# Hash attention and channel mix on one core: pair 1's preparation on VectorE with joined bits, pairs 2 and 3 with one transposing DMA each, a new order

## The chip, the cores and the metric

The kernel runs on one core of a Trainium2 chip. A core has five engines that run side by side and meet through semaphores: TensorE (PE, matrix products and transposes; its weight loads are shown as PEld), VectorE (DVE), ScalarE (ACT, exponentials and other functions), GpSimd (POOL) and SyncE (SP, which here issues nearly all DMAs). Each engine works through its own instructions in order. PE writes to PSUM, a small memory with eight banks per partition; DVE and ACT read it from there, POOL does not.

The metric is the time of one execution on the device in microseconds (us); lower is better. Three runs are given by their median. A profile is one further execution with the hardware profiler; its times count from the start of its span.

## The reference

There are 4 batches with 8 heads of 768 positions and 64 dimensions. Each row of q and of k gets a bucket: the signs of 6 projections. A score counts only where both buckets are the same. Then follow a softmax, the product with v, and a channel mix ("moe" in the names) over the 512 joined columns:

```python
q_bits = (np.einsum('bhsd,dk->bhsk', q, proj) > 0).astype(np.int64)
k_bits = (np.einsum('bhsd,dk->bhsk', k, proj) > 0).astype(np.int64)
...
mask = q_bucket[:, :, :, None] == k_bucket[:, :, None, :]
scores = scale * np.matmul(q, k.transpose(0, 1, 3, 2))
scores = np.where(mask, scores, -1000000000.0)
...
return np.matmul(attn, v).astype(np.float32)
...
xk = mu_k * x + (1.0 - mu_k) * x_prev
xr = mu_r * x + (1.0 - mu_r) * x_prev
k = np.maximum(xk @ w_k, 0.0)
v = k * k @ w_v
r = 1.0 / (1.0 + np.exp(-(xr @ w_r)))
return (r * v).astype(np.float32)
```

x is the attention output with its heads joined, x_prev is x moved on by one position. The output is float32, 4 x 768 x 512.

## The kernel before

**Pairs.** Two heads make a pair; there are 16 pairs, numbered 0 to 15, four to a batch. For each pair the kernel builds, per side (q or k) and head j, an operand `a` of 128 rows by 768 positions in float16. Its rows 0 to 63 hold four times the value rounded to float16. Its rows 64 to 127 hold, in six of them, a large positive or negative number for each of the six bits, so that the product of a q and a k column is large where all bits agree, and the exponential of any other is nothing. In pairs that are split into two float16 parts, rows 64 to 127 first get the rounded-off part ("lo"), and the six rows of bits are written over it.

**Two ways to prepare a pair.** The function `add_prep_turn` (the "turned" way) serves pairs 0 and 1. Per side: `hi` (L467, DVE) rounds to float16 into the tile `nh`; `y` (L478, PE) transposes the float32 input into PSUM; `ey` (L483, ACT) copies it out; `x` (L489, PE) multiplies it by the projection in float32; `ex` (L497, DVE) turns the results into signs inside `nh`; `t` (L512, PE, one per head) transposes `nh` into PSUM and `evt` (L517 on DVE, L519 on ACT) copies it into `a`. Pair 0 goes head by head, pair 1 with both heads of a side at once. The rest of `nh` is zero, from the memset `nz` (L265).

The function `add_prep` serves pairs 2 to 15: `hi` (L398, DVE), `lo` (L401, DVE), then a transposing DMA `tr` (L405, SP) writes `a`. Pairs 2 and 3 do this side by side (`hi2q`, `hi2k` and so on), pairs 4 to 15 (`MERGED`) with one tile for q and k together. Then `add_bits` makes the bits of all four blocks (q and k, two heads) jointly: `bits` (L427, PE, 16 products from `a`), `bx` (L431, DVE, takes the sign from PSUM into a tile), and four copies `row` (L443, POOL), one per side and head, which put six rows of bits into `a`. A score needs the rows of its own head from q and from k.

**Scores and the rest.** The scores of a pair are cut into nine steps of 1024 columns: `sc` (L544, PE) into PSUM, `exp` (L548, ACT) from there into `pt`. Steps 0 to 3 belong to head 0, step 4 to both, 5 to 8 to head 1; the order may take them in any sequence. `oo` (L571, PE, three parts per head) multiplies by v, `rc` and `ob` (L582 to L589, DVE) divide, `ot` (L599, PE) or a DMA (L605) turns the result, and the mix (L630 to L646, DVE) follows. When a batch's four pairs are mixed, its channel mix runs: `kp` (L659, PE), Relu (L663, ACT), square (L666, DVE), `r` (L679, PE) with a tanh (L682, ACT), `v` (L692, PE, two halves of four products), the last product (L699, DVE) and the store (L702, SP). v is loaded by SP (`ldv`, L335) and summed on POOL (L350 to L362); q and k by `ldq` (L330, for pair 0 L321).

**The order.** Each piece of work is added to a plan with its engine, what it reads and writes, and a PSUM bank if it takes one. The list `ORDER` then gives the sequence in which all 1332 pieces are issued, and with it the sequence on each engine and on SP's and ACT's DMA queues; the list `BANKS` gives each piece its PSUM bank. Both were written out by hand or by a planner ahead of time; nothing is reordered on the chip. Four score steps can be held in PSUM at once, fewer while other work holds banks.

At the start PE is given work on a zeroed tile until data arrive: `warm` (L246, 14 products of 256 columns) and eight `warmb` (L251, two products each), some of which stand later in the order.

Of the kernel before, what the change touches and what calls it, by code (L numbers as in the profile page):

```python
# [8 lines left out]
FP32 = mybir.dt.float32  # L9
FP16 = mybir.dt.float16  # L10
# [59 lines left out]
]  # L70

BANKS = [
# [56 lines left out]
def kernel(  # L129
# [13 lines left out]
    nc = tc.nc  # L143
# [5 lines left out]
    P = 128  # L149
# [629 lines left out]
```

## Time and profile before

| | us |
|---|---|
| median of 3 runs | 243.06 (242.08 to 243.22) |
| the profiled execution | 242.0 |
| its span, first to last instruction | 240.2 |
| busy: PE / ACT / DVE / POOL | 234.1 / 181.9 / 179.8 / 99.7 |

The granted TensorE clock was 1.00. HBM read 24.12 MB and written 6.29 MB.

In the profile's rows a group shows the line, the engine, the operation, the tiles out<-in by the program's names, and how often; then times in us (mean of one in ns). In a timeline a row shows the start, the time until the last one of the group ends, and in brackets the idle time of the engine before it and what ended it. PE's products overlap, so a row of PE ends after the next has begun. Some of PE's records can be missing from a trace. A DMA row on SP is the time of its issue; the time to landing is given in the DMA view.

### The profile page before, as it was taken

To read this page: it belongs to the slowest core of one execution; us is meant where nothing else is said; L and a number is where in the kernel's file an instruction comes from. 1 tells how busy PE (TensorE), PEld (TensorE's weight loads), DVE (VectorE), ACT (ScalarE), POOL (GpSimd) and SP (SyncE) were. 2 spreads that over 40 slices of the span, in tenths; PEclk is the share of its full clock that TensorE was granted. 3 is DMA by queue.
4 is the path that set the end of the run, shared out by engine and by line. 5 is a ranking of instruction groups with operands and counts; after the bars stand their busy time and mean duration, and the time that the engine had idled before them with its cause. 6 is when DMAs were issued, how large, how long until landed. Compare 5 with 4: busy or idle time off the path is not lost.

```text
span 240.2 us, 6251 instructions
## 1 busy us (share of the span) xinstructions
PE 234.1 (97%) x2515; PEld 147.8 (62%) x2532; DVE 179.8 (75%) x388; ACT 181.9 (76%) x242; POOL 99.7 (41%) x148
## 2 busy tenths in 40 slices
PE   8999999999999999999999999999999999999994
PEld 6985776776766565656456656665566564455442
DVE  3488789999998898989868896887167867348232
ACT  2699999999999999889779999677884640256320
POOL 4064979989934899438087302550000000000000
PEclk9999999999999999999999999999999999999999
DMA  6989999999999999988999989401500401210333
GB/s 225 304 222 274 232 242 260 279 197 362 279 253 284 273 213 294 249 302 206 276 163 241 249 177 234 136 0 26 173 0 3 120 3 44 87 46 1 131 135 131
DMA packets 72605, 44.00 MB, mean 183 GB/s; under 512 B 54912, under 2 KB 67584, under 8 KB 72576
## 3 DMA queue, kind: packets, MB, share of 16 engines
q1 hardware_dynamic: 72208, 43.20, 70.9%
q8 instruction: 20, 0.33, 0.6%
q10 hardware_dynamic: 368, 0.39, 0.5%
q14 instruction: 9, 0.07, 0.1%
HBM read 24.12 MB, written 6.29 MB: 127 GB/s over the span
## 4 chain that ended last, share of the span: by engine, by line
PE 92%; ACT 5%; issue 1%; DVE 0%
PE ps_all L544 25%; PE ps_all L692 17%; PE ps_all L659 16%; PE ps_all L571 14%; PE ps_all L679 8%; ACT pt L548 4%; PE ps_all L427 4%; PE ps_all L489 2%; PE ps_all L512 1%; PE ps_all L478 1%; ACT kr L663 1%; PE ps_all L251 1%; PE ps_all L246 1%; PE ps_all L599 1%; PE ps_all L566 1%
## 5 line engine op out<-in xcount | busy, mean ns | idle before, releaser
L548 ACT ACTIVATE pt<-ps_all 128x1024 bf16<-128x1024 f32 x144 | 138.4, 1041 | 10.9 <-PE ps_all L544 10.3
L544 PE MATMUL ps_all<-a 128*128 128x256 f16 (+1 forms) x384 | 79.2, 325 | 0.5 <-ACT pt L548 0.3
L443 POOL COPY a<-bx 6x384 f32<-6x384 f32 x56 | 38.9, 695 | 34.4 <-DVE bx L431 19.6
L544 PEld LDWEIGHTS <-a 128*128 128x128 f16 x384 | 34.0, 98 | 23.5 <-issue 4.6
L659 PE MATMUL ps_all<-xk,wk 128*128 128x384 bf16 x256 | 48.3, 326 | 0.1
L571 PEld LDWEIGHTS <-pt 128*128 128x128 bf16 x1152 | 42.5, 97 | 8.0 <-issue 0.5
L692 PE MATMUL ps_all<-wv,k 128*128 128x512 bf16 (+2 forms) x199 | 45.6, 362 | 0.5
L571 PE MATMUL ps_all<-va,pt 128*128 128x65 bf16 x1152 | 44.8, 193 | 0.0
L663 ACT ACTIVATE kr<-ps_all 128x384 bf16<-128x384 f32 x64 | 29.4, 491 | 16.0 <-PE ps_all L659 14.4
L659 PEld LDWEIGHTS <-wk 128*128 128x128 bf16 x256 | 24.2, 98 | 17.0 <-issue 0.6
L692 PEld LDWEIGHTS <-k 128*128 128x128 bf16 x208 | 19.3, 98 | 18.9 <-issue 0.3
L699 DVE SCALAR_TENSOR_TENSOR os<-rs,ps_all 128x512 f32<-128x512 f32 (+2 forms) x26 | 16.5, 643 | 19.0 <-PE ps_all L692 13.7
L682 ACT ACTIVATE rs<-ps_all 128x512 f32<-128x512 f32 x24 | 14.3, 602 | 20.5 <-PE ps_all L679 14.1
L666 DVE TENSOR_TENSOR k<-kr 128x384 bf16<-128x384 bf16 x64 | 23.2, 389 | 8.3 <-ACT kr L663 8.3
L401 DVE SCALAR_TENSOR_TENSOR nh<-nat,nh 128x1536 f16<-128x1536 f32 (+1 forms) x16 | 27.0, 1694 | 0.2
L679 PE MATMUL ps_all<-wr,xr 128*128 128x512 bf16 x88 | 23.2, 379 | 0.4
L356 POOL TENSOR_TENSOR vt<-vn 128x384 f32<-128x384 f32 x12 | 17.8, 1485 | 12.5 <-DMA vn<-in_v_dram 11.7
L589 DVE TENSOR_TENSOR ob<-ps_all,rc 128x384 bf16<-128x384 f32 x32 | 17.5, 553 | 1.4 <-DMA xt<-ob 0.8
L431 DVE TENSOR_SCALAR bx<-ps_all 128x768 uint16<-128x768 uint16 x14 | 13.4, 956 | 5.3 <-PE ps_all L427 4.7
L398 DVE TENSOR_SCALAR nh<-nat 128x1536 f16<-128x1536 f32 (+1 forms) x16 | 15.8, 985 | 0.3 <-PE ps_all L512 0.2
L679 PEld LDWEIGHTS <-xr 128*128 128x128 bf16 x96 | 9.0, 98 | 9.0
L380 DVE SCALAR_TENSOR_TENSOR va<-ps_all,vn 128x384 bf16<-128x384 f32 x24 | 12.7, 548 | 0.5 <-PE ps_all L375 0.2
(77 smaller groups left out, 188.9 us busy)
## 6 DMA issues: line engine op xcount, KB each, us to landing
vn<-in_v_dram SPq DMA_DIRECT2D x16, 384.0 KB, 5.1
out_dram<-os SPq DMA_DIRECT2D x23, 256.0 KB, 2.3
nat<-in_k_dram SPq DMA_DIRECT2D x15, 384.0 KB, 4.7
nat<-in_q_dram SPq DMA_DIRECT2D x15, 384.0 KB, 5.2
wst<-in_moe_w_k_dram SPq DMA_DIRECT2D x2, 512.0 KB, 7.0
wst<-in_moe_w_r_dram SPq DMA_DIRECT2D x2, 512.0 KB, 5.8
wst<-in_moe_w_v_dram SPq DMA_DIRECT2D x2, 512.0 KB, 4.4
k<-in_moe_w_k_dram SPq DMA_DIRECT2D x1, 512.0 KB, 4.4
```

Source lines behind the costliest of these rows:

```text
L356: e.tensor_tensor(out=vt[:, :, :, 0:E], in0=src[:, :, 0:3, 0:E], in1=src[:, :, 3:6, 0:E], op=ALU.add)
L401: nc.vector.scalar_tensor_tensor(out=nh[:, :, D:P], in0=nat.rearrange("p j (c d) -> p (j c) d", d=D), scalar=QS, in1=nh[:, :, 0:D], op0=AL ...
L443: nc.gpsimd.tensor_copy(side_a[side][n % NAQ][D : D + NB, j, :].bitcast(FP32), bx_t[sx][32 * i : 32 * i + NB, :].bitcast(FP32))
L544: nc.tensor.matmul(ps[:, lo - s * STEP : hi - s * STEP], side_a["k"][sa][:, j, jc * P : (jc + 1) * P], side_a["q"][sa][:, j, q0 : q0 + hi ...
L548: nc.scalar.activation(out=pt_t[sp][:, s * STEP : (s + 1) * STEP], in_=ps_t[plan.slot[nm]], func=AF.Exp, bias=EBIAS, scale=ESC)
L571: nc.tensor.matmul(oo[:, ic * 65 : ic * 65 + 65], pt_t[sp][:, o : o + P], va_t[sa][:, j, jc, 0 : D + 1], start=(not uc and ic == 0 and jc ...
L589: nc.vector.tensor_tensor(out=ob_t[so][:, :, j * D : (j + 1) * D], in0=oo[:, :, 0:D], in1=rc_t[sr][:, 1, :].unsqueeze(2).to_broadcast([P, ...
L659: nc.tensor.matmul(ps[:, 0:HALF], wk_sb[:, d, fc * P : (fc + 1) * P], xk_t[mx[d]][:, h * HALF : (h + 1) * HALF], start=(d == 0), stop=(d = ...
L663: nc.scalar.activation(out=kr_t[sk], in_=sm(nm)[:, 0:HALF], func=AF.Relu, scale=0.5 ** 0.5)
L666: nc.vector.tensor_tensor(out=k2_t[s2][:, h * HALF : (h + 1) * HALF], in0=kr_t[sk], in1=kr_t[sk], op=ALU.mult)
L679: nc.tensor.matmul(sm(nr), xr_t[mx[d]][:, c * P : (c + 1) * P], wr_sb[:, d, :], start=(d == 0), stop=(d == NDC - 1))
L692: nc.tensor.matmul(sm(nv)[:, x0:x1], k2_t[(b * NFC + fc) % NK2][:, c * P : (c + 1) * P], wv_sb[:, fc, x0:x1], start=(fc == 0), stop=(fc == ...
```

## The change

1. **Pair 1** leaves `add_prep_turn` (`FIRSTS` is now `(0,)`). It goes through `add_prep` side by side: `hi1q`, `lo1q`, `hi1k`, `lo1k` on DVE (L398, L401). It is in the new set `TURNED`: instead of the transposing DMA, PE transposes each head's `nh` (`t1q0` and so on) and DVE copies it out (`evt1q0` and so on). Its bits now come from `add_bits`: `bits1`, `bx1`, and four copies `row1` on POOL. So the float32 transposes, ACT's copies, the float32 products and the sign steps of pair 1 are gone.
2. **Pairs 2 and 3** join `MERGED`: one `hi`, one `lo` and one transposing DMA each, on a tile of q and k together, where there were two of each.
3. **Opening.** The tile `tb`, its memset on POOL and the small exponential named `table` on ACT are removed; `NWARM` is 8 instead of 14; the second `nh` tile is no longer zeroed; pair 0's transposes no longer name the warm products as something they wait for.
4. **`ORDER` and `BANKS`** are new throughout. The opening, read from the numbers:

```
SP before:  ldq0q0 ldq0q1 ldpw1 ldq1k ldq2k mur ldq2q ldq3k ldq1q ldv0 ldv1 ldq3q tr2q tr2k ldq4k ldv2 ldq4q muk ldv3 tr3q tr3k
SP after:   ldq0q0 ldq0q1 ldpw1 ldq1q mur ldq1k muk ldq2q ldv0 ldq2k ldv1 ldq3q ldv2 ldq3k ldq4k tr2qk ldq4q tr3qk ldv3
DVE before: wz nz0 hi0k0 hi0k1 hi0q0 ex0k0 ex0q0 hi0q1 nz1 evt0q0 ex0k1 hi1k0 ex0q1 hi2k evt0q1 hi2q lo2q lo2k ex1k0 mur hi1q0 evt1k1 hi3k ex1q0 evt1k0 evt1q1 evt1q0 hi3q lo3q bx2 lo3k hi4qk lo4qk
DVE after:  wz hi0q0 nz0 hi0k0 hi0q1 hi0k1 hi1q ex0q0 mur ex0k0 lo1q ex0k1 evt0q0 hi1k ex0q1 lo1k evt1q0 evt0q1 evt1k0 evt1k1 hi2qk evt1q1 lo2qk bx1 hi3qk rc0.0 lo3qk rc0.1 muk ob0.1 ob0.0 bx2 xt0 xs0 df0 hi4qk
PE after:   warm0-5 warmb7 warmb6 warm6 warm7 y0q0 warmb5 y0k1 y0q1 y0k0 warmb3 x0q0 x0k0 warmb2 x0k1 t0k0 t0q0 t0k1 x0q1 sc0_0 sc0_1 t1q0 t0q1 t1k0 sc0_2 t1k1 sc0_7 t1q1 sc0_5 sc0_4 sc0_3 bits1 sc0_8 oo0_0 (two parts) sc0_6 oo0_0 (third) sc1_5 sc1_7 sc1_8 oo0_1 (three) sc1_6 sc1_4 sc1_0 bits2
POOL after: ... va0 vsum0 vsum0b va1 vsum0c (2 memsets) row1k1 row1q1 row1q0 (2 memsets) row1k0 vsum1 va2 ...
```

PE's sequence before is in the timeline rows of the prediction; in the order before, pair 1 opens with score step 8, and pair 0's product with v begins behind six score steps of pair 1. At the end of the kernel the store of row block 4 of the last batch now stands between the stores of 256 to 511 and the last one, columns 0 to 255 of block 5.

The core of the diff (the two number lists left out):

```diff
-    NWARM = 14
+    NWARM = 8
...
-    MERGED = tuple(range(4, 16))
-    FIRSTS = (0, 1)
+    MERGED = tuple(range(2, 16))
+    FIRSTS = (0,)
+    TURNED = (1,)
...
-    tb = buf([P, 2], FP32, "tb")
     add("DVE", 0.2, lambda: nc.vector.memset(wz, 0.0), w=["wz"])
-    add("POOL", 0.1, lambda: nc.gpsimd.memset(tb, 0.0), w=["tb"], port=1, name="ctb")
...
-    add("ACT", 1.5, lambda: nc.scalar.activation(out=tb[:, 0:1], in_=tb[:, 1:2], func=AF.Exp), r=["tb"], w=["tb0"], at=0.75, name="table")
...
-    for i in range(NNH):
+    for i in range(1):
         add("DVE", 0.8, lambda i=i: nc.vector.memset(nh_t[i][:, :, D + NB : P].bitcast(FP32), 0.0), w=[("nz", i)], name=f"nz{i}")
...
             add("DVE", DVE_C(768 * m), lo, r=rn + nh_h, w=nh_l + [("nz", sh)], port=1, name=f"lo{n}")
+            if n in TURNED:
+                for j in range(2):
+                    nm = f"t{n}{side}{j}"
+
+                    def tp(nm=nm, nh=nh, j=j):
+                        ps = sm(nm)[:, 0:HALF].bitcast(FP16)
+                        for c in range(NSC):
+                            nc.tensor.transpose(ps[:, c * P : (c + 1) * P], nh[:, j * NSC + c, :], idh)
+
+                    def ev(nm=nm, a=a, j=j):
+                        nc.vector.tensor_copy(a[:, j, :], sm(nm)[:, 0:HALF].bitcast(FP16))
+                    add("PE", 0.48, tp, r=["idh", ("nhh", side, sh, j), ("nhl", side, sh, j)], w=[(nm,)], take=("sm", nm, 0), name=nm)
+                    add("DVE", DVE_C(S, 2), ev, r=[(nm,)], w=[("a", side, sa, j)] + [("ab", side, sa, j, h) for h in range(2)], give=[nm], name="ev" + nm)
+                continue
             add("SP", 1.86 if whole else 1.46, tr, r=nh_h + nh_l, w=ax, svc=2.95 if whole else 1.57, tr=1, name=f"tr{n}")
...
-                add("PE", 0.06 * 3 * m, tp, r=["idf", "warm", ("pt", 1, 8 * S // STEP)] + rn, w=[(ny,)], take=("sc" if whole else "sm", ny, 0), name=ny)
+                add("PE", 0.06 * 3 * m, tp, r=["idf", ("pt", 1, 8 * S // STEP)] + rn, w=[(ny,)], take=("sc" if whole else "sm", ny, 0), name=ny)
```

119 rows, old and new, of tables (BANKS, ORDER) are left out of this document.

## The prediction, made before the result was known

> **What bounds the kernel now.** I read the page's engine shares first, then the chain of work that ended last, the waits of TensorE and ScalarE, a table of windows, and the timelines of the first 60 us.
>
> ```profile
> PE 234.1 (97%) x2515; PEld 147.8 (62%) x2532; DVE 179.8 (75%) x388; ACT 181.9 (76%) x242; POOL 99.7 (41%) x148
> ...
> PE 92%; ACT 5%; issue 1%; DVE 0%
> ...
> PE ps_all L544 <- ACT pt L548: 0.3, 1, 0.3
> ...
> ACT pt L548 <- PE ps_all L544: 1.1, 4, 0.4
> ...
> 20.90:57.00 36.10, 36.07 (x585) 25.01 (x582) 33.23 (x58) 35.89 (x40) 29.64 (x35) 1.00 1.10 257
> 57.00:99.00 42.00, 41.46 (x525) 27.00 (x520) 39.09 (x82) 41.25 (x56) 32.48 (x37) 1.00 1.13 271
> 99.00:188.00 89.00, 88.47 (x920) 53.18 (x929) 68.71 (x156) 72.01 (x94) 28.03 (x43) 1.00 0.63 157
> ```
>
> TensorE (PE) is busy 234.1 of 240.2 us and has 92% of the chain, so the kernel seems simply bound by it. The windows (length, then busy PE, PEld, DVE, ACT, POOL) say more. From 99 to 188 us PE is full while ACT has 17 us of slack: there the end is set by how much PE work is left. But from 20.9 to 99 us ACT is full as well (35.89 of 36.10, 41.25 of 42.00), and its waits for PE in 19 to 99 us come to 1.1 us. In that stage two engines are full together; a microsecond taken from PE alone makes PE wait for ACT. MoE work that could fill PE needs pair 3, so it cannot come early, and in both orders the same MoE pieces stand ahead of score step 5 of pair 10 (four halves of `v0`, three of `kp1`). The PE work left at that step is the same before and after, so the end moves by what that step moves, and up to there ACT's row of exponentials sets the time:
>
> ```profile
> 10.19 0.81 ACT L483 ACTIVATE pt<-ps_all 128x768 f32<-128x768 f32 x1 [1.08 <-PE ps_all L478]
> ...
> 11.60 4.69 ACT L548 ACTIVATE pt<-ps_all 128x1024 bf16<-128x1024 f32 x5
> ...
> 16.13 0.85 ACT L483 ACTIVATE pt<-ps_all 128x768 f32<-128x768 f32 x1
> ...
> 19.06 35.03 ACT L548 ACTIVATE pt<-ps_all 128x1024 bf16<-128x1024 f32 x38 [0.24 <-PE ps_all L544]
> ```
>
> One step lasts 35.03/38 = 0.92 us. Pair 0 has nine: five in the row at 11.60, two behind the copy at 16.13, two at 19.06. The tenth, the first of pair 1, starts at 19.06 + 2 x 0.92 = 20.9. The question is when it starts after the change.
>
> **The change part by part: PE and ACT.**
>
> ```profile
> 1.59 0.85 PE L246 MATMUL ps_all<-k 128*128 128x256 bf16 x3
> ...
> 4.99 0.38 PE L246 MATMUL ps_all<-k 128*128 128x256 bf16 x2
> ...
> 8.32 0.50 PE L512 MATMUL ps_all<-idh,nh 128*128 128x128 f16 x6
> ...
> 9.30 0.85 PE L478 MATMUL ps_all<-pt,nat 128*128 128x128 f32 x6
> ...
> 10.97 0.59 PE L544 MATMUL ps_all<-a 128*128 128x512 f16 x2
> ...
> 13.59 1.51 PE L489 MATMUL ps_all<-pw,pt 128*128 128x12 f32 x12
> ...
> 14.95 0.85 PE L478 MATMUL ps_all<-pt,nat 128*128 128x128 f32 x6
> ...
> 17.18 1.41 PE L489 MATMUL ps_all<-pw,pt 128*128 128x12 f32 x12
> ...
> 39.64 0.83 PE L427 MATMUL ps_all<-a,p 128*32 128x512 f16 x16
> ```
>
> Pair 1 loses its float32 transposes and bit products: 0.85 + 0.85 + 1.51 + 1.41 = 4.62 us of PE rows, about 4.0 of PE's time since each row's end overlaps the next start by some 0.15. It gains one joined bits step, 0.83. PE is thus relieved of 3.2 us. ACT loses two copies (0.81 and 0.85). Fewer warm matmuls end the filling earlier: twelve fillers at the slow opening rate (0.85 for 3, less the overlap, 0.21 each; two stand ahead of the row at 1.59) end at 1.2 + 2.6 = 3.8, ahead of the next filler row shown; the data of pair 0 then set the start. The removed table operation, the memset of `tb` and the second memset of `nh` I cost at nothing: ACT, POOL and DVE wait for pair 0's data or for PE in the opening (the rows at 10.19 and 15.21 name such waits), and these waits cover them; were that cover gone, DVE's memset would be worth about one `lo` half.
>
> **DVE, where the work goes.** It takes over pair 1's `lo`, and it has everything else of the opening.
>
> ```profile
> nat<-in_k_dram SPq DMA_DIRECT2D x1, 384.0 KB, 4.8
> ...
> 2.27 1.09 SPq L330 DMA_DIRECT2D nat<-in_k_dram  x2
> ...
> 13.08 1.83 DVE L401 SCALAR_TENSOR_TENSOR nh<-nat,nh 128x768 f16<-128x768 f32 x2
> ...
> 15.21 0.23 DVE L497 TENSOR_SCALAR nh<-ps_all 128x72 uint16<-128x72 uint16 x1 [0.30 <-PE ps_all L489]
> 15.36 0.26 DVE L275 TENSOR_SCALAR mur<-mur 128x4 f32<-128x4 f32 x1
> 15.53 0.55 DVE L467 TENSOR_SCALAR nh<-nat 128x768 f16<-128x768 f32 x1
> ...
> 19.52 1.26 DVE L517 COPY a<-ps_all 128x768 f16<-128x768 f16 x2 [0.20 <-PE ps_all L512]
> ...
> 22.49 0.96 DVE L431 TENSOR_SCALAR bx<-ps_all 128x768 uint16<-128x768 uint16 x1 [0.24 <-PE ps_all L427]
> 23.36 0.95 DVE L401 SCALAR_TENSOR_TENSOR nh<-nat,nh 128x768 f16<-128x768 f32 x1
> 24.39 1.10 DVE L398 TENSOR_SCALAR nh<-nat 128x1536 f16<-128x1536 f32 x1
> 25.52 1.94 DVE L401 SCALAR_TENSOR_TENSOR nh<-nat,nh 128x1536 f16<-128x1536 f32 x1
> ```
>
> SP now issues q of pair 1 at 2.27, where k stood; by its row it lands 4.8 later, at 7.1. In DVE's new order `hi1q` waits for that ahead of pair 0's sign steps, so these are late: 0.55, then sign step 0.2, `mur` 0.26, sign step 0.2, `lo1q` 0.92, sign step 0.2, about 9.2 with the overlaps. PE's `t0k1` (0.50 by its row, less the overlap) and `x0q1` (half of 1.41) follow: first scores at 10.3, first exponential 0.63 later as now (10.97 to 11.60), at 10.9. That is 0.7 earlier than now. Pair 0's nine steps end at 10.9 + 9 x 0.92 = 19.2, with no copy of pair 1 between them.
>
> Is pair 1 ready at 19.2? DVE goes on: a sign step behind `x0q1` (10.7), `lo1k` 0.92 (11.6), four copies out of PSUM, the first held by PE until 11.7, at 0.5 each (13.7), `hi2qk`, now whole, 1.10 (14.8), the fifth copy (15.3), `lo2qk` whole 1.94 (17.2), `bx1` 0.96 (18.2). PE's bits step of pair 1 waits only for the fifth copy and is over by 16.4, so DVE alone sets 18.2.
>
> Then POOL copies the bits into rows (L443), and each copy must be done before a score of its head:
>
> ```profile
> 23.58 1.09 POOL L443 COPY a<-bx 6x384 f32<-6x384 f32 x1 [2.77 <-issue]
> 24.73 1.12 POOL L443 COPY a<-bx 6x384 f32<-6x384 f32 x1
> 25.91 1.92 POOL L443 COPY a<-bx 6x384 f32<-6x384 f32 x1
> 27.89 0.50 POOL L443 COPY a<-bx 6x384 f32<-6x384 f32 x1
> ```
>
> The same copy takes 0.50 or up to 1.92, and the DVE rows say when: the first ends at 24.67, 0.36 behind the `lo` that ran beside it (24.31); the second at 25.85, 0.36 behind the `hi` (25.49); the third at 27.83, 0.37 behind the whole `lo` (27.46); the fourth, beside short DVE work, takes 0.50. In the new DVE order `hi3qk` and `lo3qk` stand right behind `bx1`, with one 0.18 reciprocal between. So `hi3qk` 18.2 to 19.3 holds the first row to 19.6, and `lo3qk` 19.4 to 21.3 the second to 21.7. Score step 5 of pair 1, which opens the pair and needs both, starts at 21.7, its exponential at 22.35: 1.45 later than now. ACT stands idle from 19.2, and PE behind its waiting score: its savings are spent there. Bounds for the two rows: both free, 18.3 + 0.50 + 0.50, exponential at 20.1 (-0.8); both at 1.92, 22.9 (+2.0). I take the timed ones, as the trace shows the same neighbours.
>
> **DMA.** Pairs 2 and 3 have one transposing DMA each in place of two.
>
> ```profile
> a<-nh SPq DMA_TRANSPOSE x2, 4.0
> ...
> a<-nh SPq DMA_TRANSPOSE x1, 8.4
> ...
> 28.16 5.02 SPq L405 DMA_TRANSPOSE a<-nh  x1
> ```
>
> Today's halves of pair 2 land 4.0 after issue, a whole one 8.4 (behind loads). The whole one can start only at 17.2, so it lands between 21.2 and 25.6; PE comes to pair 2's bits at about 22.35 + 3 x 0.92 = 25.1, so it is hidden but for up to 0.5, which I keep for the upper end. SP is held 5.0 by that issue; behind it stand `ldq4q`, `tr3qk` and `ldv3`, whose v is needed ahead of pair 3's rows some ten steps later: hidden. In DVE two `hi` halves (1.1) become one (1.1), two `lo` halves 1.83 become 1.94.
>
> **The rest of the order.** Behind the tenth step the counts are the same. I credit 0.5 of ACT's 1.1 us of waits, since PE has pair 0's first head multiplied by v by then. For the new order I add 0.3, the size of the one PE wait for ACT named above (ends: 0 and 1.5, five such). At the end a 256 KB store is issued just ahead of the last one; rows of the stores:
>
> ```profile
> out_dram<-os SPq DMA_DIRECT2D x23, 256.0 KB, 2.3
> ...
> out_dram<-os SPq DMA_DIRECT2D x1, 128.0 KB, 1.7
> ```
>
> Alone, the last lands 1.7 after its issue, a big one 0.6 later than that. With the big one just ahead of it I take 0.2 more, an estimate between 0 and that 0.6.
>
> **Sum:** +1.45 - 0.5 + 0.3 + 0.2 = +1.45 us. The profiled execution took 242.0 (span 240.2); it would be 243.45. It lies 1.06 below the median of the runs, 243.06; on the median I predict 244.5.
>
> **Rivals.** *The PE saving is kept.* The page's 97% speaks for it, the full ACT against it. It decides if pair 1's second row is there by 18.5, when step 5 can follow pair 0 without a gap: the tenth step starts at 19.2, -1.7; with the credit and the store -2.0: 241.1. *It comes out even.* If only one of the two rows is held, 0.50 and 1.12, the exponential starts at 18.3 + 0.5 + 0.1 + 1.1 + 0.1 + 0.6 = 20.7, and with the rest (0) the end moves by -0.2: 242.9. *Pair 2 is late too.* `hi4qk` stands three short operations behind `bx2`; if it holds the second row of pair 2 by its 1.10, ACT waits again: 245.6. *The PE clock falls.* PE stands behind score step 5 from about 18.5 to 21.7, 3.2 us; today no such gap exists and every window has clock 1.00. At the opening, 256 columns took 0.21 at first and 0.11 later, for 3.2 us; if that comes back, 3.2 us of work take twice the time, at least 1.6 of PE: 246.1. The Trainium skill ("TensorE: Matmul & The Clock Gate", What's actually happening) says that an idle window of about 3.4 us throttles PE to half its clock; the estimated gap is just short of it, and no run here shows such a gap.
>
> **How the numbers follow.** A half per cent, 1.2 us, is about what a measurement of this kernel can tell from no change. Late rows (the forecast, 244.5) 0.36; even 0.22; saving kept 0.20; pair 2 late 0.15; clock 0.07. Faster: nearly all of the third case, 0.19. Slower: the last two and seven tenths of the first, 0.47. Same: the rest, 0.34. Range: 241.0 (the saving kept) to 246.8 (rows at 1.92 and a late pair 2).
>
> **What would show it.** Right: first exponential near 10.9, then the ninth ending near 19.2, an ACT gap of 2 to 3 us before L548 ended by PE, row copies of 1.0 to 2.2 us beside `hi` and `lo` of pair 3, and the tenth step near 22.3. Wrong: no ACT gap at 19 us (the saving kept), or PE idle past 99 us, where I see none.

## The result and the profile after

The changed kernel takes 244.02 us (median of 15 executions, 242.32 to 246.19); the kernel before took 242.74 beside it (15 executions, 242.08 to 243.7). The ratio is 1.0051, with a 95% interval of 1.0026 to 1.0075: slower by half a per cent. The profiled execution took 243.99 us, its span is 242.2 (before 242.0 and 240.2), so it is near the median. Two of the 15 executions, 244.82 and 246.19 us, had a mean TensorE clock of 0.993, the other 13 of 0.998 to 1.00; that is one of the prediction's rivals and comes up again below.

The page of the changed kernel, its shares and its chain, and the same windows as before (length, then busy PE, PEld, DVE, ACT, POOL, then the granted clock and the DMA share):

```profile
PE 232.7 (96%) x2490; PEld 144.8 (60%) x2506; DVE 183.9 (76%) x384; ACT 180.3 (74%) x239; POOL 104.2 (43%) x151
...
PE 80%; DMA 10%; DVE 3%; issue 2%; ACT 2%; POOL 1%; SPq 0%; ACTq 0%; DVEq 0%; POOLq 0%
```

```profile
11.60:20.90 9.30, 7.44 (x100) 5.01 (x98) 8.44 (x12) 7.82 (x9) 7.11 (x10) 1.00 0.74 237
20.90:57.00 36.10, 34.93 (x523) 23.75 (x526) 33.09 (x52) 34.96 (x39) 32.88 (x45) 1.00 1.12 254
57.00:99.00 42.00, 41.90 (x545) 27.48 (x540) 39.37 (x86) 41.16 (x56) 30.52 (x35) 1.00 1.09 262
99.00:188.00 89.00, 87.67 (x905) 52.35 (x913) 67.08 (x148) 70.31 (x95) 30.80 (x44) 1.00 0.72 167
```

PE now stands idle for 1.86 us of the stretch from 11.60 to 20.90 and for 1.17 of the one from 20.90 to 57, where before it was full in both. The row of before for the first stretch (that for the second, 36.07 of 36.10, is in the prediction):

```profile
11.60:20.90 9.30, 9.30 (x88) 7.30 (x86) 7.60 (x15) 9.06 (x12) 6.19 (x9) 1.00 0.91 230
```

In the chain PE has 80% (before 92%), and DMA, which had no share of note, has 10% (half of it a load of k, half a transposing DMA). From 99 to 188 us PE is idle for 1.33 (before 0.53), and 0.77 of that is one wait, the last row of PE below.

ACT's opening in the changed kernel (start, time to the end of the row's last, idle before and what ended it):

```profile
11.03 7.48 ACT L559 ACTIVATE pt<-ps_all 128x1024 bf16<-128x1024 f32 x8 [0.24 <-PE ps_all L555]
19.98 1.02 ACT L559 ACTIVATE pt<-ps_all 128x1024 bf16<-128x1024 f32 x1 [1.48 <-PE ps_all L555]
21.47 7.62 ACT L559 ACTIVATE pt<-ps_all 128x1024 bf16<-128x1024 f32 x8 [0.46 <-PE ps_all L555]
```

The first exponential comes at 11.03 (before 11.60). Pair 0's first eight follow in one row, but ACT waits 1.48 for the ninth, and the tenth, pair 1's first, starts at 21.47 where it was 20.89. The other three engines of the changed kernel in that stretch say why:

```profile
15.86 2.27 DVE L398 SCALAR_TENSOR_TENSOR nh<-nat,nh 128x1536 f16<-128x1536 f32 x1
18.05 0.94 DVE L442 TENSOR_SCALAR bx<-ps_all 128x768 uint16<-128x768 uint16 x1
18.92 0.94 DVE L395 TENSOR_SCALAR nh<-nat 128x1536 f16<-128x1536 f32 x1
20.42 0.20 DVE L593 RECIPROCAL rc<-ps_all 128x6 f32<-128x6 f32 x1 [0.56 <-PE ps_all L582]
20.53 1.86 DVE L398 SCALAR_TENSOR_TENSOR nh<-nat,nh 128x1536 f16<-128x1536 f32 x1
```

```profile
16.48 1.92 POOL L359 TENSOR_TENSOR vsu<-vt 128x130 bf16<-128x130 f32 x1
...
19.14 1.09 POOL L454 COPY a<-bx 6x384 f32<-6x384 f32 x1 [0.61 <-DVE bx L442]
20.28 0.50 POOL L454 COPY a<-bx 6x384 f32<-6x384 f32 x1
20.84 1.92 POOL L454 COPY a<-bx 6x384 f32<-6x384 f32 x1
```

```profile
18.45 0.33 PE L577 MATMUL ps_all<-vsu,tiny 128*128 128x390 bf16 x1 [1.09 <-POOL vsu L359]
...
20.84 1.46 PE L555 MATMUL ps_all<-a 128*128 128x256 f16 x8 [0.53 <-POOL a L454]
...
103.45 0.83 PE L438 MATMUL ps_all<-a,p 128*32 128x512 f16 x16 [0.77 <-DMA a<-nh]
```

DVE's whole `lo2qk` (15.86 to 18.13) holds the last small sum over v of pair 0 on POOL (L359, 1.92) until 18.40; the same sum took 0.42 in the timeline of before (L362 there):

```profile
18.47 0.42 POOL L362 TENSOR_TENSOR vsu<-vt 128x130 bf16<-128x130 f32 x1
```

The product with v (L577) waits for it, and score step 6 of pair 0 stands behind that on PE: so the ninth exponential is late. `hi3qk` (to 19.86) holds the first row copy of pair 1 (1.09, to 20.23). The second takes 0.50, because the reciprocal `rc0.0` waited for PE until 20.42 and `lo3qk` could not start before 20.53; the third, which no early score needs, is held to 22.76.

The same opening starts its exponentials at different times in different executions (11.60 in the kernel before, 12.91 in b_wl6, whose opening is the same), so a run is best read from its own first exponential. The table gives, from the trace of every run but b_copies_dve (its opening stalls, see below), the start of the first exponential, then the time from there to the start of the 10th, 46th and 91st exponential and to the end of PE's last product; the last column is the ratio to the kernel before with its interval.

| run | first | 10th | 46th | 91st | PE's end | ratio |
|---|---|---|---|---|---|---|
| before | 11.60 | 9.29 | 42.71 | 96.47 | 225.08 | 1 |
| after | 11.03 | 10.44 | 44.51 | 98.76 | 227.59 | 1.0051 (1.0026 to 1.0075) |
| b_pe_cut | 11.56 | 8.84 | 42.37 | 97.06 | 225.66 | 0.9997 (0.9977 to 1.0017) |
| b_wl6 | 12.91 | 9.29 | 42.71 | 97.57 | 226.18 | 1.0026 (1.0007 to 1.0046) |
| b_merge | 12.28 | 9.29 | 43.64 | 97.78 | 226.38 | 1.0048 (1.0013 to 1.0084) |
| a_bits10 | 10.29 | 10.26 | 44.60 | 99.74 | 228.59 | 1.0049 (1.0019 to 1.0078) |
| a_sc06 | 11.37 | 9.78 | 43.85 | 98.75 | 227.57 | 1.0060 (1.0028 to 1.0091) |
| a_wl6 | 11.20 | 9.46 | 43.55 | 97.56 | 226.39 | 1.0051 (1.0027 to 1.0075) |
| a_wl6_sc06 | 11.04 | 11.45 | 46.52 | 100.52 | 229.35 | 1.0074 (1.0042 to 1.0106) |
| a_hi3 | 11.37 | 8.89 | 44.07 | 98.04 | 226.87 | 1.0026 (1.0005 to 1.0046) |
| a_best | 10.18 | 9.10 | 44.66 | 98.07 | 226.89 | 1.0032 (1.0011 to 1.0053) |
| a_halves | 11.17 | 10.13 | 43.84 | 97.86 | 227.33 | 0.9989 (0.9967 to 1.0012) |
| a_new | 10.42 | 10.09 | 43.83 | 97.24 | 225.88 | 0.9972 (0.9951 to 0.9993) |

Names with a `b` start from the kernel before, those with an `a` from the changed one. Before and after, piece by piece: -0.57 at the first exponential, +1.15 to the tenth, +0.65 to the 46th, +0.49 to the 91st, +0.22 to PE's end: +1.94. That is more than the 1.28 between the medians, since the profiled execution of before (242.0) was one of its faster ones. So in these two traces the changed kernel starts its exponentials earlier and loses four times that behind the first one (2.51 us), nearly half of it by the tenth.

### The profile page after: what moved, and what is told of

Read it like the earlier page. It is cut to its first block, busy times and chain, and to the rows that moved or that the text cites. A ratio compares the mean times of both kernels' runs of the same rounds, so it can differ in the third digit from the quotient of the medians.

```text
span 242.2 us, 6201 instructions
## 1 busy us (share of the span) xinstructions
PE 232.7 (96%) x2490; PEld 144.8 (60%) x2506; DVE 183.9 (76%) x384; ACT 180.3 (74%) x239; POOL 104.2 (43%) x151
## 4 chain that ended last, share of the span: by engine, by line
PE 80%; DMA 10%; DVE 3%; issue 2%; ACT 2%; POOL 1%; SPq 0%; ACTq 0%; DVEq 0%; POOLq 0%
PE ps_all L555 22%; PE ps_all L670 17%; PE ps_all L703 16%; PE ps_all L582 12%; PE ps_all L690 8%; DMA nat<-in_k_dram 5%; DMA a<-nh 5%; PE ps_all L438 4%; ACT pt L559 2%; DVE nh L398 1%; PE ps_all L610 1%; POOL a L454 1%; DVE nh L395 0%; DVE xk L646 0%; DVE bx L442 0%
## 5 line engine op out<-in xcount | busy, mean ns | idle before, releaser
L555 PE MATMUL ps_all<-a 128*128 128x512 f16 (+1 forms) x384 | 79.5, 325 | 1.2 <-POOL a L454 0.5
L454 POOL COPY a<-bx 6x384 f32<-6x384 f32 x60 | 44.2, 736 | 34.0 <-DVE bx L442 17.3
L703 PE MATMUL ps_all<-wv,k 128*128 128x512 bf16 (+2 forms) x200 | 46.1, 362 | 0.4
L677 DVE TENSOR_TENSOR k<-kr 128x384 bf16<-128x384 bf16 x64 | 24.1, 392 | 17.5 <-ACT kr L674 17.4
L398 DVE SCALAR_TENSOR_TENSOR nh<-nat,nh 128x1536 f16<-128x1536 f32 (+1 forms) x16 | 28.4, 1778 | 0.2
L353 POOL TENSOR_TENSOR vt<-vn 128x384 f32<-128x384 f32 x12 | 17.1, 1425 | 9.8 <-DMA vn<-in_v_dram 6.8
L442 DVE TENSOR_SCALAR bx<-ps_all 128x768 uint16<-128x768 uint16 x15 | 14.3, 955 | 3.8 <-PE ps_all L438 2.0
L438 PE MATMUL ps_all<-a,p 128*32 128x256 f16 (+1 forms) x240 | 13.1, 328 | 1.0 <-DMA a<-nh 0.8
```

What stands on the lines that cost most here:

```text
L398: nc.vector.scalar_tensor_tensor(out=nh[:, :, D:P], in0=nat.rearrange("p j (c d) -> p (j c) d", d=D), scalar=QS, in1=nh[:, :, 0:D], op0=AL ...
L438: nc.tensor.matmul(ps[32 * i : 32 * i + 32, lo:hi], w_, side_a[side][m % NAQ][:, j, lo:hi], start=(x == 0), stop=(x == len(mats) - 1))
L454: nc.gpsimd.tensor_copy(side_a[side][n % NAQ][D : D + NB, j, :].bitcast(FP32), bx_t[sx][32 * i : 32 * i + NB, :].bitcast(FP32))
L555: nc.tensor.matmul(ps[:, lo - s * STEP : hi - s * STEP], side_a["k"][sa][:, j, jc * P : (jc + 1) * P], side_a["q"][sa][:, j, q0 : q0 + hi ...
L677: nc.vector.tensor_tensor(out=k2_t[s2][:, h * HALF : (h + 1) * HALF], in0=kr_t[sk], in1=kr_t[sk], op=ALU.mult)
L703: nc.tensor.matmul(sm(nv)[:, x0:x1], k2_t[(b * NFC + fc) % NK2][:, c * P : (c + 1) * P], wv_sb[:, fc, x0:x1], start=(fc == 0), stop=(fc == ...
```

## The experiments

**What TensorE's saving alone is worth.** In the kernel before, pair 1's float32 transposes and bit products are replaced by short bf16 products on the zeroed tile. Pair 1's bits are not computed in this run; everything else is as before. In the expectations of this and the next three runs, W is the prediction's account (ACT's row and the waits around it set the time), P that PE's work sets it.

```diff
 pair 1 of the kernel before, y (L478) and x (L489)
-    six float32 transposes of 128 columns per head; six float32 products of 12 columns per head
+    one bf16 product of 512 and one of 256 columns; one of 12 * NB columns
```

> The kernel before, with pair 1's float32 transposes and bit products each replaced by one or two short bfloat16 products on the zero tile (so pair 1's bits are not computed): about 3.6 us less work on PE, nothing else moved. Theory W (ScalarE's row of exponentials sets the time up to about 99 us, so PE work saved in the opening is mostly lost to waiting): the end moves by -0.4 to -1.0 us, as far as the first exponential moves. Rival P (PE at 97% bounds everything): the end moves by -3.0 to -3.6 us.

Measured: 242.45 us, ratio 0.9997. Neither the 3.0 us of P nor even W's small gain arrived. The tenth exponential is 0.45 earlier, the 46th 0.34, and the 91st 0.59 later than before: PE waits at 94.8 us for pair 9's row copies, which POOL did not have ready. A view of the waits and of the timeline of that run:

```profile
PE ps_all L551 <- POOL a L443: 0.8, 1, 0.8
```

```profile
95.54 1.46 PE L551 MATMUL ps_all<-a 128*128 128x512 f16 x8 [0.75 <-POOL a L443]
```

**Pair 1's copies from ACT to DVE,** to relieve ACT alone:

```diff
-                ("ACT" if n == 0 else "ACT",      # engine of ey
+                ("ACT" if n == 0 else "DVE",
```

> The kernel before, with pair 1's two copies out of PSUM (0.81 and 0.85 us) on VectorE instead of ScalarE; PE work is unchanged. Theory W: ScalarE's row becomes 1.66 us shorter ahead of the tenth step; the end moves by -0.8 to -1.6 us. Rival P: 0, within 0.3 us.

Measured: 248.45 us, ratio 1.0221 (1.0181 to 1.0262), a plain miss. The copy `ey1` stands in DVE's order where its input isn't there yet, and a part of pair 0's preparation is queued behind it. So the run says nothing on ACT, but it shows what a gap on PE costs. Timeline and windows of this run:

```profile
9.93 0.96 DVE L485 TENSOR_SCALAR pt<-ps_all 128x768 f32<-128x768 f32 x1 [1.96 <-PE ps_all L478]
...
12.45 0.51 PE L512 MATMUL ps_all<-idh,nh 128*128 128x128 f16 x6 [2.56 <-DVE nh L497]
```

```profile
10.00:15.00 5.00, 2.55 (x23) 1.88 (x24) 3.97 (x10) 1.73 (x2) 0.32 (x1) 0.92 0.87 311
15.00:20.00 5.00, 5.00 (x35) 3.77 (x34) 4.75 (x7) 3.97 (x5) 4.76 (x7) 0.74 0.28 55
```

PE waits 2.56 us, and its clock falls to a mean of 0.92 and then 0.74 in the two windows shown: the clock rival's mechanism.

**Two waits of the changed kernel, one at a time.** First the late one: PE waits at 102.7 us for pair 10's transposing DMA, with MoE work behind it that could go ahead.

```diff
 PE order of the changed kernel
-  bits10 sc9_6 sc9_7 v0_1_0.1 oo9_1.0
+  v0_1_0.1 bits10 sc9_6 sc9_7 oo9_1.0
```

> The changed kernel with four products of v0_1 (0.86 us) put ahead of pair 10's bits step, in front of which PE waits 0.93 us for the transposing DMA at 102 us. Theory W: past 99 us PE alone sets the end, so the wait is filled and the end moves by -0.7 to -0.9 us. Rival: the next step of pair 10 takes the wait over and the end stays, within 0.3 us.

Then the early one, the score step behind POOL's sum:

```diff
 PE order of the changed kernel
-  oo0_0.0 oo0_0.1 sc0_6 oo0_0.2 sc1_5
+  sc0_6 oo0_0.0 oo0_0.1 oo0_0.2 sc1_5
```

> The changed kernel with score step 6 of pair 0 put ahead of pair 0's first product with v, which waits for a sum on GpSimd until 18.45 us. Theory W (pair 1's rows hold the tenth step): the ninth exponential comes at 18.4 to 18.9 instead of 19.98, the tenth stays near 21.4, the end stays within 0.4 us. Rival V (this wait for the sum is what costs the opening): the tenth comes at 20.0 to 20.5 and the end moves by -1.0 to -1.5 us.

Measured: 243.76 and 244.40 us, ratios 1.0049 and 1.0060 where the changed kernel has 1.0051: neither moved the time further than the intervals reach. In the first the wait only changed its place (0.45 at `bits10`, 0.68 for ACT behind it). In the second the tenth exponential is 0.66 nearer to the first (9.78 against 10.44) and the 46th as well, but at pair 10 all of it is spent: PE comes to `bits10` earlier and waits longer.

```profile
103.77 0.83 PE L438 MATMUL ps_all<-a,p 128*32 128x512 f16 x16 [1.42 <-DMA a<-nh]
```

**The load ahead of pair 10.** In the changed kernel the load of MoE weights `wl6` (512 KB) stands with two others directly ahead of pair 10's transposing DMA; before, it was issued 20 us earlier. SP's rows of the changed kernel (start, time of the issue):

```profile
89.84 0.57 SPq L294 DMA_DIRECT2D k<-in_moe_w_v_dram  x1
90.52 0.98 SPq L294 DMA_DIRECT2D wst<-in_moe_w_v_dram  x2
91.78 7.26 SPq L402 DMA_TRANSPOSE a<-nh  x1
```

The issue takes 7.26 (before 4.56), and it lands at 103.40 (before 101.24). Three runs move the load:

```diff
 SP order: a_wl6 and a_wl6_sc06 (the second with sc0_6 moved as well)
-  ldq9k ldv7 otd4 wl4 ldq10k ... otd6 wl6 wl9 wl8 tr10qk
+  ldq9k ldv7 otd4 wl4 wl6 ldq10k ... otd6 wl9 wl8 tr10qk
 SP order: b_wl6 (its cast wc6 moves on POOL to ahead of wc8)
-  ldq9k wl6 ldq10k ... otd6 wl8 wl9 otd7 tr10qk
+  ldq9k ldq10k ... otd6 wl6 wl8 wl9 otd7 tr10qk
```

> The changed kernel with one load, wl6 (512 KB of MoE weights), back between ldq9k and ldq10k, where the kernel before has it, and no longer between otd6 and the transposing DMA of pair 10. Theory Q (what pair 10 needs from the DMA queue sets the end, so that the opening is given back there): in the changed kernel tr10qk lands at 103.40 and PE waits 0.93 for it; one 512 KB load less ahead of it should land it 1.2 to 1.6 earlier (wl9 to wl8 landed 1.35 apart), near 102, the transposing DMA otd7 behind it as well (now 104.01), so that DVE's bx10 no longer stands behind it; the wait of bits10 goes and exp10_5 comes near 108.8 (now 109.79): the time falls by 0.9 to 1.4, the ratio to the kernel before near 1.000. The prediction's theory O (the opening alone set the loss, 0.6 to 1.2 at the tenth to the 46th step): the time does not move, ratio 1.005.

> As the run before, and score step 6 of pair 0 ahead of the multiplication by v that waited for POOL's sum. Alone, that step's move brought the ninth exponential 1.3 forward and the end nothing. Theory Q: with pair 10 no longer late, a part of it is now kept: 0.2 to 0.8 below the run with wl6 alone, ratio 0.997 to 0.999. Theory O, and any theory by which a gain of the opening dies before pair 10: the same as the run with wl6 alone, within 0.2.

> The kernel before with wl6 moved to behind otd6 and its cast wc6 to ahead of wc8, as the changed kernel has them; the opening is untouched. Theory Q: tr10qk, now landing at 101.24 with bits10 at 103.48, lands about 1.3 to 2.0 later, near 103, and otd7 (97.14) near 98.5; bits10 barely waits, so the end moves by 0 to +1.0. Theory O: 0. A result above +0.5 says that the place of this load is part of the loss; a result of 0 leaves open whether the load only hurts together with the other order of otd7.

Measured: a_wl6 243.65 us, 1.0051; b_wl6 243.64, 1.0026; a_wl6_sc06 244.86, 1.0074. In the trace of a_wl6 the wait at `bits10` is gone and PE's end is 1.20 nearer to its first exponential, but the time did not fall: two intervals of 0.0024 to either side allow no more than 0.0034 of the ratio, 0.8 us. In the kernel before, the move cost 1.0026; in its trace PE waits 0.87 for `wv`, which the cast on POOL writes, and for no transposing DMA. So the place of this load can cost some tenths of a microsecond, but undoing it in the changed kernel gave nothing back that the intervals can show, and it isn't the whole of the loss. The theory that pair 10 alone pins the end fell here.

a_wl6_sc06 showed something else. Its rows for POOL, DVE, PE and ACT, and its windows:

```profile
18.70 1.09 POOL L454 COPY a<-bx 6x384 f32<-6x384 f32 x1 [0.61 <-DVE bx L442]
19.84 1.96 POOL L454 COPY a<-bx 6x384 f32<-6x384 f32 x1
...
19.72 1.72 DVE L398 SCALAR_TENSOR_TENSOR nh<-nat,nh 128x1536 f16<-128x1536 f32 x1
...
21.85 1.47 PE L555 MATMUL ps_all<-a 128*128 128x256 f16 x8 [2.35 <-POOL a L454]
...
22.48 1.94 ACT L559 ACTIVATE pt<-ps_all 128x1024 bf16<-128x1024 f32 x2 [3.06 <-PE ps_all L555]
```

```profile
20.00:25.00 5.00, 3.15 (x37) 2.44 (x37) 1.44 (x1) 2.52 (x3) 4.74 (x9) 0.82 1.05 215
25.00:30.00 5.00, 4.91 (x51) 2.71 (x49) 3.03 (x7) 3.76 (x5) 2.46 (x7) 0.84 1.08 214
```

This is the case the prediction described, within 0.13 us: `lo3qk` now starts at 19.72, 0.12 ahead of the second row copy, and holds it to 21.80 (forecast 21.7); the exponential starts at 22.48 (forecast 22.35). Behind PE's gap of 2.35 the mean clock is 0.82 and then 0.84 in the two windows shown. Whether `lo3qk` or the copy starts first is decided by a tenth of a microsecond, so the same kernel can fall on either side. In the trace of a_bits10, whose opening has the same order, the first row copy took 0.50 and the second 1.14, which is the case of the prediction's second rival. A mean clock of 0.990 to 0.993 was seen in 12 of the 63 executions of the changed kernel and of a_bits10, a_sc06, a_wl6 and a_wl6_sc06, which all keep that order, and in none of the 48 of a_halves, a_hi3, a_best and a_new. Only this one of the 12 was profiled; that the other 11 have the same cause is likely, and not shown.

**The merge of pairs 2 and 3,** alone in the kernel before, and undone in the changed kernel:

```diff
 b_merge (whole operations at the places of hi2q lo2k tr2k and of hi3q lo3q tr3q)
-    MERGED = tuple(range(4, 16))
+    MERGED = tuple(range(2, 16))
 a_halves (the halves side by side at the places of the whole ones)
-    MERGED = tuple(range(2, 16))
+    MERGED = tuple(range(4, 16))
```

> The kernel before with pairs 2 and 3 merged alone: one hi, one lo and one transposing DMA of 768 KB for q and k, each at the place of the first half's hi, second half's lo and first half's DMA; the opening of pairs 0 and 1 as before. The prediction costed the merge at nothing (hidden up to 0.5): ratio 1.000, within 0.002. Rival (the whole DMA of pair 2 lands too late): it lands 3 to 4 later than the halves did, PE waits for it ahead of bits2, and if that is kept the ratio is 1.003 to 1.005.

> The changed kernel with pairs 2 and 3 in halves again (hi, lo and transposing DMA for q and for k, 4 DVE operations more, 2 DMAs more), everything else as the change has it. In the kernel before, the merge alone cost 1.0048. Theory M (merging is the loss): the two halves of pair 2 land earlier than 23.71, bits2 no longer waits 0.8, and the ratio comes to 0.999 to 1.002. Theory P/Q (the rows of pair 1 and pair 10 set it, the merge cost there only because the whole lo3qk stood ahead of bx2): 1.003 to 1.006.

Measured: b_merge 243.94 us, ratio 1.0048 (1.0013 to 1.0084); a_halves 242.48 us, 0.9989 (0.9967 to 1.0012). The merge alone costs what the whole change costs, and without it the change costs nothing that could be measured; the intervals of after and of a_halves don't touch. Counted from the first exponential, b_merge loses 0.93 by the 46th exponential and 1.30 by PE's end. The place, in its timeline:

```profile
21.38 1.03 DVE L397 TENSOR_SCALAR nh<-nat 128x1536 f16<-128x1536 f32 x1
22.45 1.76 DVE L400 SCALAR_TENSOR_TENSOR nh<-nat,nh 128x1536 f16<-128x1536 f32 x1
24.13 0.95 DVE L430 TENSOR_SCALAR bx<-ps_all 128x768 uint16<-128x768 uint16 x1
...
25.13 0.59 PE L543 MATMUL ps_all<-a 128*128 128x256 f16 x3 [0.97 <-DVE bx L430]
```

It is not the DMA's landing, as my rival had it: in that trace PE waits for no transposing DMA. Where one half of `hi3` and of `lo3` stood ahead of `bx2` (0.55 and 0.96 before), the whole ones now stand there, and `bx2` with PE behind it is 0.97 late. The two halves in the kernel before:

```profile
20.70 0.55 DVE L398 TENSOR_SCALAR nh<-nat 128x768 f16<-128x768 f32 x1
21.28 0.96 DVE L401 SCALAR_TENSOR_TENSOR nh<-nat,nh 128x768 f16<-128x768 f32 x1
```

A merge with the whole `lo3qk` behind `bx2` was not tried, so a part of these 1.0048 may belong to the place that was chosen for it. In the changed kernel the order is another, and there the whole operations hold POOL; no PE product waits for a transposing DMA there ahead of pair 10's, so the landing of the whole ones isn't the loss there either. In a_halves the same sum of POOL took 0.73 and PE did not wait for it:

```profile
14.68 0.73 POOL L359 TENSOR_TENSOR vsu<-vt 128x130 bf16<-128x130 f32 x1
...
17.67 0.33 PE L577 MATMUL ps_all<-vsu,tiny 128*128 128x390 bf16 x1
...
19.20 1.02 ACT L559 ACTIVATE pt<-ps_all 128x1024 bf16<-128x1024 f32 x1 [0.31 <-PE ps_all L555]
21.30 27.75 ACT L559 ACTIVATE pt<-ps_all 128x1024 bf16<-128x1024 f32 x30 [1.08 <-PE ps_all L555]
```

ACT's wait ahead of the ninth step falls from 1.48 to 0.31, and from the tenth on the row has 30 steps without a break. The halves are not all of that difference: here the sum started at 14.68, ahead of `lo2q` (16.33). Among the seven traces with the whole operations it took 1.92 in five, and 1.12 and 1.21 in a_sc06 and a_hi3, where it also started ahead of `lo2qk` and ended 0.27 behind `hi2qk`; in a_new, with halves and beside `lo2q`, it took 1.12. The profiled execution of a_halves was its longest of 12 (243.8 us, with 0.76 us of PE lost ahead of 118.01 in a wait for a transposing DMA), so its trace doesn't show the size of the gain, and how the 1.5 us divide between POOL's sum, pair 2's bits and the executions with the slower clock stays open.

**The half-precision step of pair 3 behind the reciprocal,** alone and with the two other moves:

```diff
 DVE order of the changed kernel (a_hi3, a_best)
-  bx1 hi3qk rc0.0 lo3qk
+  bx1 rc0.0 hi3qk lo3qk
 a_best also: wl6 as in a_wl6, sc0_6 as in a_sc06
```

> The changed kernel with the half-precision step of pair 3 (hi3qk) moved in DVE's order from right behind bx1 to behind the reciprocal rc0.0 of pair 0's first head, so that nothing long runs on DVE beside the first two row copies of pair 1. Theory P (a long DVE operation holds POOL's row copies; where lo3qk holds the second one, PE waits over 2 us and its clock falls): row1k1 and row1q1 take 0.50 each (1.09 and 0.50 in the changed kernel, 1.09 and 1.92 in the run with both other moves), the tenth exponential comes 0.4 to 0.6 earlier than 21.47 at the same ninth, and no execution shows the mean clock of 0.990 to 0.993 that 2 of 15 executions of the changed kernel and 3 to 5 of 12 of its variants show; the median falls by 0.3 to 0.8, ratio 1.001 to 1.004, and the highest executions (over 245.5) are gone. Theory Q (pair 10 pins the end): the fast executions stay where they are, 1.004 to 1.005.

> All three moves together: wl6 back between ldq9k and ldq10k, score step 6 of pair 0 ahead of the multiplication by v that waits for POOL's sum, hi3qk behind rc0.0. Theory P: the 2.5 us wait of PE for the second row of pair 1 (run with wl6 and step 6) is gone, the ninth exponential comes near 18.4, the tenth near 19.6, PE's clock is 1.00 in every execution, and with pair 10 no longer late (no wait at bits10 in the run with wl6) the opening is kept: 242.3 to 243.0, ratio 0.998 to 1.001. Theory Q without a cure at pair 10: 1.003 to 1.005, with a new wait between 85 and 110 us. If the saving of TensorE were kept whole, 240.5: I do not expect it.

Measured: a_hi3 243.12 us, 1.0026; a_best 243.47, 1.0032. Both row copies take 0.50, the tenth exponential is 1.55 and 1.34 nearer to the first than in the changed kernel, no execution is above 244.51 and none has the slower clock. But most of it is given back by the 46th (0.44 nearer, and 0.15 farther): the largest of PE's new waits behind the tenth is for the identity `idb` of the next transposes, which POOL makes behind the row copies. A timeline row of a_hi3 and one of a_best:

```profile
25.41 0.50 PE L610 MATMUL ps_all<-idb,ob 128*128 128x128 bf16 x6 [0.80 <-POOL idb masks.py:199]
```

```profile
24.79 0.49 PE L610 MATMUL ps_all<-idb,ob 128*128 128x128 bf16 x6 [0.81 <-POOL idb masks.py:199]
```

a_hi3's interval overlaps that of the changed kernel, so a gain is likely and not shown; a_best's expected 0.998 to 1.001 was missed.

**A version of both.** Pair 1 turned as the change has it, halves for pairs 2 and 3, and three moves:

```diff
 from a_halves
-  DVE: bx1 hi3q hi3k rc0.0 lo3q lo3k
+  DVE: bx1 rc0.0 hi3q hi3k lo3q lo3k
-  POOL: idb behind pair 1's row copies
+  POOL: idb ahead of them (ahead of cxz5 cva1 row1k1)
-  SP: otd6 wl6 wl9 wl8 tr10qk
+  SP: wl6 ahead of ldq10k
```

> The changed kernel with pair 1 turned as the change has it, but pairs 2 and 3 in halves (the run that came to 0.9989), and three small moves: both half-precision steps of pair 3 behind the reciprocal rc0.0, the identity idb made on POOL ahead of pair 1's row copies, and wl6 back between ldq9k and ldq10k. Theory M (the merge is the loss, and the turn of pair 1 by itself is worth what the waits leave of it): row1k1 and row1q1 take 0.50 each, the 1.3 us wait of PE ahead of pair 1's first score falls below 0.7, the waits for idb (0.8) and at bits10 (0.7) are gone: 0.4 to 1.2 below the run with halves, ratio 0.994 to 0.998. Rival (nothing of the opening is kept past pair 10): the same as the run with halves, 0.999.

Measured: 242.21 us (241.39 to 242.91) beside 243.04 for the kernel before in the same comparison, ratio 0.9972 (0.9951 to 0.9993): faster than both kernels, by 0.3% than the kernel before. Against a_halves (0.9989) the intervals overlap. The second row copy took 0.72 rather than 0.50, and PE's wait ahead of pair 1's first score did not fall below 0.7:

```profile
19.87 1.46 PE L555 MATMUL ps_all<-a 128*128 128x256 f16 x8 [1.25 <-POOL a L454]
```

PE comes there earlier and waits for `bx1` and its rows, which DVE sets; but from 20.50 on ACT has 22 steps in 20.45 us without a gap, PE does not wait at `bits10`, and its end stands 1.71 nearer to the first exponential than in the changed kernel.

## Why the prediction came out as it did

The prediction was 244.5 us and slower; the time is 244.02 us, 1.28 above the kernel before in the same comparison where the sum had +1.45. The size is right, but its parts are not.

- *The saving of PE is spent in waiting*: right. b_pe_cut shows it without the rest of the change (0.9997 with PE relieved), and the windows of after show where it went: 1.86 + 1.17 us of idle PE ahead of 57 us.
- *First exponential at 10.9*: right (11.03; 10.18 to 11.37 over the runs of this kind, 11.56 to 12.91 over four of the old kind).
- *Pair 0's nine steps end at 19.2*: wrong, the ninth began at 19.98. The prediction let DVE's operations hold pair 1's row copies on POOL, and not the other POOL work beside a whole `lo`. It left out that PE's order puts `sc0_6` behind a product that needs POOL's sum.
- *DVE alone sets 18.2, the end of `bx1`*: it ended at 18.99. `hi2qk` and `lo2qk`, costed at 1.10 and 1.94 us, took 1.47 and 2.27.
- *`hi3qk` holds the first row to 19.6, `lo3qk` the second to 21.7*: the first half right (1.09, to 20.23), the second wrong here: the text called the reciprocal between them "one 0.18", but it waits for PE, and by that the second copy got through. a_wl6_sc06 fell on the other side and gave the forecast numbers. So the tenth step came at +0.58 and not +1.45.
- *Behind the tenth step the counts are the same* (-0.5 + 0.3 + 0.2 = 0): the step that failed. From the tenth exponential to PE's end it is +1.36. The store's 0.2 was 0: from PE's last product to the end of the span it is 3.55, before 3.53.
- *The transposing DMA of a whole pair is hidden but for up to 0.5; two halves become one of about the same length*: the term that was mis-sized, and the largest. Costed at nothing, it is worth 1.0048 alone and 0.0062 of the ratio when undone. What was overlooked is not the DMA but that an operation twice as long cannot be passed: `bx2` waits for the whole of it in b_merge (0.97 on PE), and POOL does in the changed kernel (1.92 for the sum). The price of the merge is measured; that these holds are all of it in the changed kernel is argued and not shown.
- *Wrong if PE is idle past 99 us*: it is (0.77 at 103.45), so by the prediction's own mark the end isn't set by the tenth step alone. Gains of the opening did not reach the end in a_sc06.
- *The clock rival* (0.07): its mechanism happens, in a_wl6_sc06 from a gap of 2.35 us rather than 3.2, and by the mean clock in 2 of 15 executions of the changed kernel. There it adds 0.2 us to the mean of the 15 (244.17 against 243.96 without these two), so it isn't the cause of the result.
- *Range to 246.8*: its own parts (+2.0 with both rows at 1.92, 1.10 for a late pair 2, up to 0.5 for the DMA) give 246.2 to 246.7; the result is far from that end.

Since the two mis-sized terms (-0.87 at the tenth step, +1.36 behind it) nearly cancel, the close number is partly luck. These parts are those of the two traces, whose spans differ by 2.0 (242.2 and 240.2) where the medians differ by 1.28, so each size holds only to some tenths of a microsecond.

## What to carry to other kernels

Before merging two operations into one of the same total length, look for what stands behind them in their engine's order and for what runs meanwhile on an engine that they hold up (here POOL): the sum of the durations stays, the longest hold doubles. Where two engines are full together, count a saving on one of them as waiting until a run with that saving alone says otherwise. And when an order depends on which of two operations starts first by a tenth of a microsecond, price both outcomes, since executions will show both.

## What the runs showed of the hardware

A small POOL operation that starts beside a long `hi` or `lo` on DVE doesn't slow down in proportion; it ends a fixed time behind it. The row copies ended 0.37 behind `hi3qk` and 0.37 behind `lo3qk` in the changed kernel (20.23 and 19.86; 22.76 and 22.39), 0.36 in a_wl6_sc06 (21.80 and 21.44), and the sum over v 0.27 behind `lo2qk`, whether they take 0.42 or 0.50 alone. The copy that had started 0.25 ahead of `lo3qk` in the changed kernel took its 0.50. With halves, in a_halves and a_new, the longest of pair 1's row copies took 1.11 and 0.91 in place of 1.92. The Trainium skill ("SBUF — State Buffer", Who interferes with whom) calls the port the two engines share an exclusive lock, held for the whole instruction. These rows agree with that.

The clock fell behind gaps of PE of 2.35 and 2.56 us, and not at once. Windows of a_wl6_sc06 and of b_copies_dve, two each, set at the times at which the recorded clock changes: the 3.4 us with the gap or the most of it, and the next 3.4:

```profile
19.76:23.16 3.40, 1.31 (x9) 0.88 (x10) 1.68 (x2) 0.68 (x1) 3.12 (x6) 1.00 1.11 194
23.18:26.57 3.39, 3.39 (x42) 2.67 (x41) 0.90 (x4) 2.16 (x3) 3.22 (x8) 0.50 1.08 264
...
10.81:14.21 3.40, 1.76 (x20) 1.43 (x21) 2.54 (x8) 0.94 (x2) 0.00 (x0) 1.00 0.95 352
14.23:17.62 3.39, 3.39 (x14) 1.84 (x12) 3.18 (x5) 2.49 (x3) 2.86 (x3) 0.50 0.08 26
```

In both, PE was busy for 1.31 and 1.76 us of a stretch of 3.4 at full clock, then the granted clock was 0.50 for the next 3.4, though PE was at work all that time, and 1.00 behind it. The Trainium skill ("TensorE: Matmul & The Clock Gate", What's actually happening) gives half speed behind an idle window of about 3.4 us. The length and the speed in these rows agree with that. A wholly idle stretch was not needed here: those ahead had PE busy for 39% and 52%.
